# Attention and feed-forward layer on one core: three jobs of exponentials kept in SBUF during the lead-in, with V made afterwards

## The chip, the cores and the metric

The kernel runs on one core of a Trainium2 chip. The metric is the device time of one execution in microseconds (us). Engines are named as in the profile: PE is TensorE (PEld its weight loads), ACT is ScalarE, DVE is VectorE, POOL is GpSimd, SP the engine that issues the DMAs.

## What is computed

A transformer layer in bfloat16, 2048 tokens, model width 1024, 32 heads of 32, hidden width 3584:

```python
x  = A_x                                            # [1, 2048, 1024]
qkv = layernorm(x) @ wqkv                           # no affine part in the norm
p  = softmax(q @ k.T * 32 ** -0.5)                  # per head, all 2048 keys, no mask
h  = x + (p @ v) @ wo
h2 = h + gelu(layernorm(h) @ w1 + b1) @ w2 + b2     # gelu by tanh
```

## The kernel before

**Tasks and a planner.** The Python code adds tasks to a graph (`Graph.add`): each has an engine, the instructions it emits, a planned duration (`occ`), a latency until its result can be used (`lat`), buffers read and written, a priority and a kind. `Graph.schedule` plays the graph through with these durations and so fixes, before the run, the order of instructions on every engine; on the chip each engine works through its list in order and waits on semaphores. PE's next task is chosen by `pick_pe`: score matmuls (`qk`) first, then PV and its sums where enough rounds wait (`PV_FORCE`, `PV_START`), then everything else (`bg`: projections, output projection, feed-forward), by order of creation. Other engines take the ready task with the lowest priority number, then the earliest created. A change of the tiling mode of PE (full, row, col) is planned with `switch`. Planned durations are `MM` for a matmul of 512 columns, `c_dve`, `c_dve_ps`, `c_act` and a few literals.

**Attention.** Heads are taken in 8 blocks `g` of four (32 rows or columns of PE each), queries in 8 blocks `qb` of 256. A job is one (qb, g) and has 8 rounds of 256 keys. A round (`Att.qk`, line 769) makes the scores of four heads in two score units of two PSUM banks each; two ACTIVATEs of 1024 elements (line 779) write their exponentials to one of NR = 9 buffers PT. `Job.pv` (line 805) multiplies V by them into the left half of a bank, DVE adds the two key halves of a PT buffer (a pair sum, PS, line 820, three buffers), and `Job.den` (line 834) sums over the keys with a matmul by ones. `Job.finish` (lines 850 to 865) divides and writes one block of OT. In all there are 64 jobs, 512 rounds and 1024 exponentials.

**Lead-in.** x comes in 16 tiles of 128 tokens; in 8 steps `hc` of two tiles: layer norm on DVE and POOL (lines 583 to 598), transposes on PE (line 604), copy to xnT on ACT (line 611) or DVE (line 613), then Q (for hc < 2) and K of block 0 for these 256 tokens (`proj_half`), V of blocks 0 and 1 (`proj_v`, line 706), and the rounds of jobs (0,0) and (1,0) that have become possible. In this stage the scores use two units (banks 0 to 3); the two jobs hold banks 5 and 6, and the projections share banks 4 and 7. PV follows two rounds behind (`LEAD_LAG`), and these two jobs sum directly from PT, without pair sums. 80 matmuls with no use for the result (line 1007, kind `warm`) are there for moments in which PE has nothing else.

**Afterwards** there are three score units (banks 0 to 5), and jobs and projections share banks 6 and 7 (`slot`). For each g from 1 to 7: Q of query chunk 0, K of all tokens, V of a later block (`rest_of_projections`), then jobs (0,g) and (1,g), and for g in `EXTRA` also (2,g). K and Q go through DVE (line 654). Then follow the rest of Q (`late_q`), and for each query block the output projection `wo`, `ln2`, `ffn1`, `gelu`, `ffn2`, with the jobs three query blocks ahead between them. `wo(u)` needs all eight jobs of query block u, and its first matmul uses g = 7. The last query block is a tail after all attention. Most full-width matmuls are recorded at lines 534 (four column tiles) and 537 (whole), those of the tail at line 540. Line 558 issues nearly all DMAs.

## Time and profile before

| | |
|---|---|
| device time, 3 runs | median 1102.87 us (1101.98 to 1104.28) |
| span of the profiled execution, first to last instruction | 1099.2 us |
| busy: PE, DVE, ACT, POOL | 1056.5, 757.2, 1019.8, 47.8 us |
| exponentials (line 779) | 1024, 953.6 us busy |
| DMA | 174.43 MB, mean 159 GB/s |

The profiled execution is one run of the program. Its own time is its span and what lies around the first and the last instruction; the page gives the span alone, and the median of the runs lies 3.7 us above that. A busy time counts overlapping instructions of an engine once, so that a matmul that waits in the pipeline counts as busy PE; the mean duration of one instruction is its latency, and can be longer than its distance to the next.

### The profile page before, as it was taken

Reading aid. Unit: us, or ns where it says so; the run is one execution under the profiler, and the core shown is the slowest. Engines: PE = TensorE matmul, PEld = TensorE weight load, DVE = VectorE, ACT = ScalarE, POOL = GpSimd, SP = SyncE. Lnnn points to the kernel's source line nnn. Section 1 sums busy time; section 2 is a strip of 40 time slices with the busy share of each in tenths; the row PEclk is TensorE's granted clock in tenths of the full one; section 3 lists DMA queues with packets and bytes.
Section 4 is the critical chain, followed back from the end, with each engine's and each line's share of the span. In section 5 each row is a group of like instructions: output and inputs, shape, how many; then the busy total and the mean of one; then the engine's idle time right before and its main releaser. Section 6 shows DMA issues by size and latency. Waiting matters only on the chain.

```text
span 1099.2 us, 42056 instructions
## 1 busy us (share of the span) xinstructions
PE 1056.5 (96%) x19177; PEld 613.8 (56%) x19226; DVE 757.2 (69%) x1444; ACT 1019.8 (93%) x1124; POOL 47.8 (4%) x110
## 2 busy tenths in 40 slices
PE   8899999998899999999999899999999999999998
PEld 6655555553345744664475456546744664565483
DVE  7746666665676886788588768876886787687501
ACT  3879999999999999999999999999999999999650
POOL 3200000000000001001000100010010000000100
PEclk9999999999899999999999999999999999999999
DMA  6820000048345654854576466448654747797370
GB/s 184 227 103 2 29 2 3 2 159 268 115 122 154 189 151 150 260 162 149 185 228 188 150 203 180 143 150 255 181 178 149 216 142 239 243 266 242 98 262 20
DMA packets 265506, 174.43 MB, mean 159 GB/s; under 512 B 26864, under 2 KB 260336, under 8 KB 264560
## 3 DMA queue, kind: packets, MB, share of 16 engines
q1 hardware_dynamic: 265328, 171.74, 51.2%
q8 instruction: 151, 2.47, 0.9%
q14 instruction: 27, 0.22, 0.1%
HBM read 161.23 MB, written 10.49 MB: 156 GB/s over the span
## 4 chain that ended last, share of the span: by engine, by line
ACT 79%; PE 19%; DVE 1%; issue 0%; DMA 0%; POOL 0%; POOLq 0%; DVEq 0%
ACT PT L779 75%; PE ps L540 6%; ACT uu L965 4%; PE ps L537 4%; PE ps L534 3%; PE ps L769 2%; PE ps L805 1%; PE ps L1007 1%; PE ps L834 1%; DMA a_w1r<-in_A_wo_dram 0%; ACT xnT L611 0%; PE ps L604 0%; DVE PS L820 0%; DVE OD L850 0%; DVE OD L857 0%
## 5 line engine op out<-in xcount | busy, mean ns | idle before, releaser
L779 ACT ACTIVATE PT<-ps 128x1024 bf16<-128x1024 f32 x1024 | 953.6, 1189 | 18.2 <-PE ps L769 18.0
L820 DVE TENSOR_TENSOR PS<-PT 128x1024 bf16<-128x1024 bf16 x434 | 287.5, 686 | 124.5 <-ACT PT L779 63.8
L769 PE MATMUL ps<-QT,KT 32*128 32x256 bf16 x4096 | 204.6, 273 | 13.5 <-ACT PT L779 10.2
L805 PE MATMUL ps<-PT,V 128*32 128x256 bf16 x4096 | 179.9, 273 | 1.5 <-ACT PT L779 1.1
L769 PEld LDWEIGHTS ps<-QT,KT 32*128 32x128 bf16 x4096 | 61.0, 92 | 174.1 <-ACT PT L779 165.3
L834 PE MATMUL ps<-PS,ones 128*32 128x256 bf16 x1736 | 121.7, 274 | 2.0 <-DVE PS L820 2.0
L805 PEld LDWEIGHTS ps<-PT,V 128*32 128x32 bf16 x4096 | 103.8, 97 | 30.0 <-issue 8.7
L537 PE MATMUL ps<-a_w2r,gT 128*128 128x512 bf16 x445 | 109.6, 380 | 4.9 <-issue 2.4
L537 PE MATMUL ps<-hnT,a_w1r 128*128 128x256 bf16 x903 | 111.2, 273 | 1.1 <-DVE rr L860 0.5
L534 PE MATMUL ps<-hnT,a_w1r 128*32 128x256 bf16 x2660 | 96.9, 274 | 2.4 <-DVE gT L943 1.2
L537 PEld LDWEIGHTS ps<-hnT,a_w1r 128*128 128x128 bf16 x903 | 82.7, 98 | 25.1 <-issue 14.8
L943 DVE TENSOR_TENSOR gT<-ps,b1f 128x512 bf16<-128x512 f32 x98 | 67.3, 687 | 27.7 <-PE ps L534 18.4
L534 PE MATMUL ps<-a_w2r,gT 128*32 128x512 bf16 x1140 | 81.6, 381 | 2.5 <-DVE OD L857 2.5
L534 PEld LDWEIGHTS ps<-hnT,a_w1r 128*32 128x32 bf16 x2660 | 66.2, 96 | 18.5 <-issue 14.0
L537 PEld LDWEIGHTS ps<-a_w2r,gT 128*128 128x128 bf16 x471 | 40.4, 98 | 55.3 <-issue 15.7
L989 DVE SCALAR_TENSOR_TENSOR hch<-ps,hch 128x512 bf16<-128x512 f32 x32 | 22.0, 689 | 64.0 <-PE ps L540 47.1
L834 PEld LDWEIGHTS ps<-PS,ones 128*32 128x32 bf16 x1736 | 45.9, 96 | 22.8 <-issue 8.7
L965 ACT ACTIVATE uu<-uu 128x1024 bf16<-128x1024 bf16 x49 | 58.0, 1206 | 0.0
L537 PE MATMUL ps<-xnT,Wall 128*128 128x512 bf16 (+1 forms) x213 | 47.7, 360 | 2.3 <-issue 1.1
L588 POOL CAST mvb<-mv 128x2 bf16<-128x2 f32 (+1 forms) x25 | 6.1, 242 | 990.0 <-DVE mv L585 987.2
L706 DVE CAST V<-ps 128x512 bf16<-128x512 f32 x32 | 22.1, 690 | 30.8 <-PE ps L537 15.8
L537 PE MATMUL ps<-Wall,xnT 128*128 128x256 bf16 x327 | 41.0, 273 | 0.0
(85 smaller groups left out, 1009.8 us busy)
## 6 DMA issues: line engine op xcount, KB each, us to landing
a_w2r<-in_B_w_dram SPq DMA_DIRECT2D x105, 512.0 KB, 5.6
a_w1r<-in_B_w_dram SPq DMA_DIRECT2D x98, 512.0 KB, 4.4
a_w1r<-in_A_wo_dram SPq DMA_DIRECT2D x32, 512.0 KB, 4.0
b_w1r<-in_B_w_dram SPq DMA_DIRECT2D x14, 512.0 KB, 5.8
a_w1r<-in_A_wqkv_dram SPq DMA_DIRECT2D x11, 512.0 KB, 4.3
xrb<-in_A_x_dram SPq DMA_DIRECT2D x16, 256.0 KB, 4.2
Wall<-in_A_wqkv_dram SPq DMA_DIRECT2D x16, 256.0 KB, 4.8
hch<-in_A_x_dram SPq DMA_DIRECT2D x16, 256.0 KB, 4.0
```

Source lines behind the costliest of these rows:

```text
L534: fns.append(lambda p, j=j: p.matmul(psum[32 * j:32 * j + 32, bi(bank), c0:c1], lhsT[:, 32 * j:32 * j + 32], rhs, start=start, stop=stop, ...
L537: t.whole = lambda p: p.matmul(psum[:, bi(bank), c0:c1], lhsT, rhs, start=start, stop=stop, skip_group_check=True)
L540: t = pe(lambda p: p.matmul(psum[:, bi(bank), c0:c1], lhsT, rhs, start=start, stop=stop), occ, reads=reads, writes=[bb(bank)], mode="full" ...
L706: t = dve(lambda v: v.tensor_copy(dst, psum[:, bi(bank), :].rearrange("p (t g c) -> p g t c", t=2, g=2)), c_dve_ps(512), reads=[bb(bank)], ...
L769: return p.matmul(psum[:, 2 * us[h // 2] + h % 2, 256 * i:256 * i + 256], KT[32 * h:32 * h + 32, g, k0:k0 + P], QT[32 * h:32 * h + 32, qs, :],
L779: act(lambda a, u=u, k=k: a.activation(PT[:, s, k, :, :], psum[:, 2 * u:2 * u + 2, :], ACT.Exp, bias=0.0, scale=SCALE), 1024, reads=[B_ps[ ...
L805: fns.append(lambda p, i=i, h=h: p.matmul(psum[32 * h:32 * h + 32, bi(bank), 0:256], V[:, g, 2 * r + i, 32 * h:32 * h + 32], PT[:, s, h // ...
L820: dve(lambda v: v.tensor_tensor(PS[:, n, :, :], pairs[:, :, 0:256], pairs[:, :, 256:512], ALU.add), c_dve(1024, 2), reads=[B_PT[2 * s], B_ ...
L834: fns.append(lambda p, h=h, rhs=rhs, i=i: p.matmul(psum[32 * h:32 * h + 32, bi(bank), 256:512], ones32[:, :], rhs, start=False, stop=last, ...
L943: t = dve(lambda v: v.tensor_tensor(g[:, fc:fc + 2, :], psum[:, bi(bank), :].rearrange("p (f c) -> p f c", f=2), b1f[:, fc:fc + 2].unsquee ...
L965: act(lambda a: a.activation(w, w, ACT.Tanh, bias=0.0, scale=KT2), 1024, reads=[B_uu[i]], writes=[B_uu[i]], prio=-1)
L989: drop(dve(lambda v, hs=hs, bank=bank, half=half: v.scalar_tensor_tensor(hch[:, hs, c], psum[:, bi(bank), :], half, hch[:, hs, c], ALU.mul ...
```

## The change

The lead-in now works on three jobs, (0,0), (1,0) and (2,0), with three score units from the start, and makes only scores and exponentials. V of block 0 is made in four slots of four tiles (`proj_v1`), and PV of these jobs is held back until the last of them is cast (`gate`); their pair sums wait for the last DVE task of the lead-in (`hold`). The exponentials of the 24 rounds stay in SBUF: eight in PT, sixteen in further buffers (`extra_pt`) that lie where K and V of blocks 2 to 5, V of block 1 and weight blocks 5, 3 and 1 go later, and in free space. ACT copies tiles 0 to 3 to xnT and DVE the other twelve; before, ACT copied tiles 0 to 8, 10, 12 and 14. V of block 1 is made in `rest_of_projections(1)`, after `gate`. `EXTRA` becomes [1, 2], so that (2,1) comes early too, as (2,2) did. All lead-in jobs use pair sums for seven of their eight rounds. The order in which two V weight loads stand in SP's list changes, and most of the planner's durations and latencies get other values.

```diff
-    def schedule(self, pick_pe, pool, switch=0.1, dma_rate=280.0, dma_lat=2.1, dma_issue=0.06):
+    def schedule(self, pick_pe, pool, switch=0.104, dma_rate=280.0, dma_lat=2.1, dma_issue=0.06):
...
+    PTs = [PT[:, i] for i in range(NR)]
+    B_PTs = [B_PT[2 * i:2 * i + 2] for i in range(NR)]
...
+    def extra_pt(off):
+        i = len(PTs)
+        h, b = sb(Area(off), "PX%d" % i, [P, 2, 2, 512], BF, 2)
+        PTs.append(h)
+        B_PTs.append(b)
+
+    for g in (2, 3, 4, 5):
+        extra_pt(B_KT[8 * g].lo)
+        extra_pt(B_V[NT * g].lo)
+    for k in (5, 3, 1):
+        extra_pt(B_W[k][0].lo)
+        extra_pt(B_W[k][0].lo + 4096)
+    extra_pt(ph0.cur)
+    extra_pt(B_V[NT].lo)
...
-    MM = 0.2195
+    MM = 0.21333
     def c_dve_ps(n):
-        return (120 + n) / 960.0 + 0.02
+        return (120 + n) / 960.0 - 0.058
     def c_dve(n, x=1):
-        return (62 + n / x) / 960.0 + 0.085
+        return (62 + n / x) / 960.0
     def c_act(n, ap_bias=False):
-        return 0.073 + (0.093 if ap_bias else 0.0) + n / 1200.0
+        return (0.064 if n == 1024 else 0.073) + (0.093 if ap_bias else 0.0) + n / 1200.0
...
-        occ = MM * (c1 - c0) / 512.0 + 0.003
+        occ = MM * (c1 - c0) / 512.0 + 0.0026
...
-            if r == 7 or (self.g == 0 and self.qb < 2):
+            if r == 7:
                 self.sums.append((s, True))
...
-                    reads=[B_PT[2 * s], B_PT[2 * s + 1]], writes=[B_PS[n]], prio=-2)
+                    reads=B_PTs[s], writes=[B_PS[n]], prio=-2, after=hold if self.g == 0 and self.qb < NLJ else ())
...
-    load_w(WV, -5, 0, 256)
     for tt in range(4, 8):
         x_tile(tt, -5)
+    load_w(WV, -5, 0, P)
...
-    LEAD_LAG = 2
-    lead_jobs = [Job(0, 0, 6), Job(1, 0, 5)]
-    att.n_units = 2
+    LEAD_ACT = (0, 1, 2, 3)
+    NLJ = 3
...
-            tr_tile(tt, lead_slot(), "dve" if tt >= 8 and tt % 2 else "act")
+            tr_tile(tt, slot(), "act" if tt in LEAD_ACT else "dve")
...
     for hc in range(8):
         ev = "act" if hc == 0 else "dve"
-        if hc < 2:
-            proj_half(0, hc, lead_slot(), ev)
-        proj_half(1, hc, lead_slot(), ev)
-        first = [t for t in gr.tasks if t.kind == "bg"][-1:] if hc == 0 else ()
+        if hc < NLJ:
+            proj_half(0, hc, slot(), ev)
+        proj_half(1, hc, slot(), ev)
         if hc < 7:
             lead_norm(hc + 1)
-        proj_v(2 * hc, 0, lead_slot(), ev, first)
-        for k, r in {0: [(0, 0)], 1: [(0, 1), (1, 0), (1, 1)]}.get(hc, [(0, hc), (1, hc)]):
-            s = att.qk((k, 0), r)
-            pending.append((lead_jobs[k], r, s))
-            attention_drain(LEAD_LAG)
-    attention_drain()
-    att.n_units = 3
...
+        for k, r in [(k, hc) for k in range(min(hc, NLJ))] + ([(hc, r) for r in range(hc + 1)] if hc < NLJ else []):
+            n = 8 * k + r
+            s = NR + 15 if n == 0 else n - 1 if n < 9 else n
+            lead_rounds.append((k, r, att.qk((k, 0), r, s)))
+    att.rounds = 8
+    hold = [t for t in gr.tasks if t.eng == E.DVE][-1:]
+    for c in range(4):
+        proj_v1(4 * c, 0, 4, slot(), "dve", 0, True)
+    gate = gr.tasks[-1]
+    for k in range(NLJ):
+        job = Job(k, 0, slot(2))
+        for _, r, s in [x for x in lead_rounds if x[0] == k]:
+            job.pv(r, s)
...
+        if g == 1:
+            for c in range(4):
+                proj_v1(4 * c, 1, 4, slot(), "dve", 0, True, [gate])
+        if g in EXTRA:
+            proj(0, g, 1, slot(), "dve")
...
-    EXTRA = [2]
+    EXTRA = [1, 2]
...
-    attention(2, [g for g in range(G) if g not in EXTRA])
+    attention(2, [g for g in range(1, G) if g not in EXTRA])
...
     def ready_rounds(now):
...
+        if gate.done is None or gate.done > now + 1e-9:
+            return 0
```

## The prediction

> **What bounds the kernel now.** I read the page first, then the busy time by stretch, the chain of waits, and the lead-in by form and in order of time.

> ```profile
> span 1099.2 us, 42056 instructions
> ...
> PE 1056.5 (96%) x19177; PEld 613.8 (56%) x19226; DVE 757.2 (69%) x1444; ACT 1019.8 (93%) x1124; POOL 47.8 (4%) x110
> ...
> ACT 79%; PE 19%; DVE 1%; issue 0%; DMA 0%; POOL 0%; POOLq 0%; DVEq 0%
> ```

> ACT carries 79% of the chain that ends last. Where it does not is read from the stretches (all engines, then the exponentials of line 779 alone):

> ```profile
> 0.00:23.00 23.00, 20.13 (x176) 16.11 (x177) 15.39 (x35) 7.97 (x9) 8.60 (x26) 1.00 0.78 206
> 23.00:71.20 48.20, 43.83 (x1059) 30.51 (x1058) 31.21 (x72) 35.88 (x38) 9.07 (x20) 1.00 0.67 194
> 71.20:272.00 200.80, 196.06 (x3598) 109.72 (x3610) 125.08 (x225) 200.79 (x220) 0.00 (x0) 1.00 0.19 59
> 285.00:1031.00 746.00, 722.16 (x13812) 414.15 (x13840) 567.49 (x1079) 743.60 (x809) 26.72 (x56) 1.00 0.61 185
> 1031.00:1099.20 68.20, 64.77 (x434) 40.29 (x439) 11.49 (x23) 19.43 (x37) 3.40 (x8) 1.00 0.37 125
> ...
> 0.00:23.00 23.00, 1.94 (x2) 1.00 0.78 206
> 23.00:71.20 48.20, 29.35 (x30) 1.00 0.67 194
> ```

> The columns are PE, PEld, DVE, ACT, POOL, granted clock, DMA share, GB/s. From 71.2 to 1031 ACT is busy almost throughout. Two stretches are left: the lead-in to 71.2, in which ACT finishes only 32 exponentials (2 + 30), and the 68.2 us tail of feed-forward matmuls, which the change leaves alone. In the middle PE has almost as little room as ACT: 722.2 of 746 us. So ACT sets the pace and PE is close behind. Both matter below.

> The profiled execution has a span of 1099.2 us; the median of the runs is 1102.87, so 3.7 us are added to every span below.

> **The lead-in on ACT.** The chain of waits, and ACT in order of time:

> ```profile
> 71.21 208.25 ACT PT L779 x227
> ...
> 16.40 1.94 ACT L779 ACTIVATE PT<-ps 128x1024 bf16<-128x1024 f32 x2 [0.62 <-PE ps L769]
> 19.97 1.02 ACT L611 ACTIVATE xnT<-ps 128x1024 bf16<-128x1024 bf16 x1 [0.71 <-PE ps L604]
> 24.82 1.02 ACT L779 ACTIVATE PT<-ps 128x1024 bf16<-128x1024 f32 x1 [3.82 <-PE ps L769]
> 40.49 1.94 ACT L779 ACTIVATE PT<-ps 128x1024 bf16<-128x1024 f32 x2 [0.51 <-PE ps L769]
> ```

> Back to back, one exponential takes 208.25/227 = 0.917 us, a round of two 1.834. In the lead-in ACT waits about 0.51 us for the scores before a round (two score units, both occupied), and it also copies transposed tiles: 12 of them, 12.2 us in the row further down.

> After the change ACT keeps tiles 0 to 3 (4 copies, all done by 21 us in the trace of before) and the score units become three, as they are already from 71.2 on, where no such wait is left. The first round can hardly move from 16.4 us, since it hangs on the first two x tiles. The second key chunk came at 24.8; with V's matmuls out of the way I put it at 23, an estimate. From there ACT has 48 − 2 = 46 exponentials and no copy: 46 × 0.917 = 42.2 us, so three jobs are done at 65.2. At 71.2 that makes 48 + 6.0/0.917 = 54.5 exponentials against 32. The 22.5 more are worth 22.5 × 0.917 = **20.6 us**, if ACT is fed without a gap.

> [...] The trace has 0.917, and the sum goes by that.

> **Can DVE feed it?** The lead-in by form, up to 71.2 us:

> ```profile
> L583 DVE BATCH_NORM_STATS2 st<-xrb 128x6 f32<-128x512 bf16 x32 | 21.2, 671 | 4.3 <-DMA xrb<-in_A_x_dram 4.3
> L598 DVE TENSOR_SCALAR xb<-xrb,mvr,rden 128x1024 bf16<-128x1024 bf16 x16 | 8.0, 534 | 0.6 <-POOL rden L594 0.5
> L706 DVE CAST V<-ps 128x512 bf16<-128x512 f32 x8 | 5.5, 690 | 11.1 <-PE ps L534 5.9 <-PE ps L537 5.1
> L585 DVE BATCH_NORM_AGGREGATE mv<-st 128x2 f32<-128x12 f32 x16 | 3.3, 207 | 0.4
> L743 DVE CAST KT<-ps 128x256 bf16<-128x256 f32 x7 | 3.0, 425 | 5.0 <-PE ps L534 4.3 <-PE ps L537 0.5
> L613 DVE COPY xnT<-ps 128x1024 bf16<-128x1024 bf16 x4 | 2.8, 688 | 0.4 <-PE ps L604 0.2
> L611 ACT ACTIVATE xnT<-ps 128x1024 bf16<-128x1024 bf16 x12 | 12.2, 1034 | 10.1 <-PE ps L604 10.1
> ```

> Layer norms: 21.2 + 8.0 + 3.3 = 32.5 us, and about 1 for the small casts. Copies: 12 × 0.688 = 8.3 instead of 4. K and Q casts of block 0: 9 × 0.425 = 3.8. Together 45.6, and 4.3 us of waiting for x, so the last key chunk is ready at 50 us at the earliest. If four V casts and five casts of block 1's Q and K (9 × 0.69 = 6.2) fall in between, at 56. ACT needs that chunk for its last six exponentials, at 65.2 − 5.5 = 59.7. So moving eight copies to DVE costs nothing as long as DVE stays under 59.7; the cover is some 4 us, and each microsecond beyond it is lost on ACT.

> **Handing over to block 1.** From the page, from SP's queue, and PE in the middle of the projections:

> ```profile
> L820 DVE TENSOR_TENSOR PS<-PT 128x1024 bf16<-128x1024 bf16 x434 | 287.5, 686 | 124.5 <-ACT PT L779 63.8
> ...
> 29.76 20.92 SPq L558 DMA_DIRECT2D Wall<-in_A_wqkv_dram  x17
> ...
> 180.48 0.40 PE L769 MATMUL ps<-QT,KT 32*128 32x256 bf16 x8
> 180.81 1.68 PE L537 MATMUL ps<-xnT,Wall 128*128 128x512 bf16 x7
> 182.43 0.40 PE L769 MATMUL ps<-QT,KT 32*128 32x256 bf16 x8
> ```

> Block 1's weights are issued from 29.8 us on, and the lead-in now has no PV and only a little V to hold up PE, so its Q and K can be done before 65. Behind the last V cast wait 24 rounds of PV, and the pair sums wait for the last K cast of the lead-in; what queues behind both is the sums' matmuls on PE and the closings on DVE, and the projections of block 1 that need a bank. The rounds are bound by DVE: 21 pair sums (seven a job) of 0.686 = 14.4 us, and three closings. Meanwhile two jobs hold banks 6 and 7, and the third takes the first that is freed. If V is complete at 57, projections get a bank at about 69 and both at 75. V of block 1 is 32 matmuls' worth of 512 columns; seven such take 1.68 us in the row above, and a following score matmul starts 0.10 us after the last, so about 0.217 each, 6.9 us in all, with half of PE free 13 us: ready at 82. ACT goes on without it for as long as PT has buffers, 9 rounds × 1.834 = 16.5 us, to 81.7. Bounds: 0 (V of block 1 gets in early) and 6 us (it starts only at 75). I take **2 us**, nearer to zero because the two times all but meet.

> SP's queue: V's weights change place with x tiles, and blocks 1, 3 and 5 of the weights wait for their place in SBUF to be read out by PV, at about 75 us; they are for blocks 4 to 7, over 90 us later (a block is two jobs, 29.3 us). I cost both at nothing.

> **PE from the first output projection on.** PE in order of time, then two stretches:

> ```profile
> 277.67 0.61 PE L769 MATMUL ps<-QT,KT 32*128 32x256 bf16 x8 [0.30 <-ACT PT L779]
> 279.50 0.61 PE L769 MATMUL ps<-QT,KT 32*128 32x256 bf16 x8 [1.22 <-ACT PT L779]
> 280.05 2.31 PE L537 MATMUL ps<-a_w1r,OT 128*128 128x512 bf16 x5
> ...
> 275.00:280.00 5.00, 2.67 (x52) 0.86 (x52) 2.81 (x7) 5.00 (x6) 0.00 (x0) 0.76 0.48 144
> 280.00:285.00 5.00, 5.00 (x24) 1.50 (x20) 1.98 (x3) 4.13 (x5) 0.00 (x0) 0.56 0.01 3
> ```

> Here PE ran out of projections and idled until job (0,7) was complete, for only then can the output projection start. Before that point lie 16 jobs; with three early jobs of block row 2 they are 18. Before: 71.2 + 14 × 14.67 = 276.6, first matmul at 280.05. After: 65.2 + 15 × 14.67 = 285.3, so 288.7. PE starts its long part 8.7 us **later**. It then has 16 rounds less beside it. A round takes PE 0.43 (scores with both changes of mode) + 0.22 (PV, as many columns as one matmul of 512 in 0.217) + 0.11 (pair sums, half of that), 0.77 us: 16 × 0.77 = 12.3. At an unchanged pace PE would be only 3.6 us earlier at the end, and ACT's gain needs 17 us more from PE's 746.

> Is that there? Rows of the stretch 285 to 1031:

> ```profile
> L769 PE MATMUL ps<-QT,KT 32*128 32x256 bf16 x3040 | 151.4, 273 | 8.1 <-ACT PT L779 6.2
> L537 PE MATMUL ps<-hnT,a_w1r 128*128 128x256 bf16 x903 | 111.2, 273 | 1.1 <-DVE rr L860 0.5 <-DVE OD L857 0.3
> L537 PE MATMUL ps<-a_w2r,gT 128*128 128x512 bf16 x441 | 108.6, 380 | 4.9 <-issue 2.4 <-DVE gT L967 1.1 <-DVE hch L989 0.7
> L534 PE MATMUL ps<-hnT,a_w1r 128*32 128x256 bf16 x2660 | 96.9, 274 | 2.4 <-DVE gT L943 1.2 <-issue 1.0
> L534 PE MATMUL ps<-a_w2r,gT 128*32 128x512 bf16 x1140 | 81.6, 381 | 2.5 <-DVE OD L857 2.5
> ```

> PE's visible idle is 746 − 722.2 = 23.8 us, 8.1 of it before score matmuls. The order is computed with 0.2195 + 0.003 us for a matmul of 512 columns, and it takes 0.217; these rows hold about 451 + 441 + 332 + 285 = 1509 of them, so the order leaves 1509 × 0.0055 = 8.3 us unused, and the new number (0.2159) fills that. The change of mode is planned at 0.104, close to what the rows show. So 8 to 17 of the 17 us can be found. I take 13, between the two, and lose **4 us**. ACT's shift of durations itself (0.926 planned, 0.917 measured) costs no instruction and I give it nothing.

> Pair sums instead of direct sums for two lead-in jobs save PE 14 × 0.11 = 1.5 us; it lies in the slack above.

> Sum: 1099.2 − 20.6 + 2 + 4 = 1084.6; with 3.7, **1088 us**.

> **The rivals.**
> 1. *ACT alone decides.* PE finds all 17 us and the handover costs nothing: 1078.6 + 3.7 = 1082. For it: 23.8 us of visible idle. Against: these lie scattered, and some wait for DVE. Chance 0.21.
> 2. *PE becomes the bound.* Nothing is found: 1099.2 − 3.6 + 3.7 = 1099. For it: PE already 97% busy there. Against: the 8.1 us in which PE waits for ACT vanish by themselves when ACT is ahead. Chance 0.14.
> 3. *Bank lock-out, slower.* Block 1's Q and K do not get through the two banks before the backlog of PV takes both. ACT then has nothing from 65.2 until a bank frees at 69 and Q and the first K are made (2 × 1.75 us and casts): 75, 10 us. V of block 1 comes after K, at about 95, and PT is full at 91.5: 4 more. PE idling in that time comes back at half clock, as at 280 to 285 (0.56): Q, K and V of block 1, 5 × 1.74 + 6.9 = 15.6 us, take up to twice as long, 10 us of it uncovered. 24 + 4 (PE) − 20.6 = 7 slower: 1110. It decides from 20.6 − 4 = 16.6 us of ACT drought on. Against: weights are there from 30 us. Chance 0.17. [...]

> That lead-in buffers in KT and V delay block 2's projections is part of rival 3's mechanism and not counted again.

> **How the numbers follow.** Forecast (1084 to 1095) 0.45, rivals 0.21, 0.14 and 0.17, and 0.03 that cases cancel to no change. About 2.2 us (0.2%) is what a measurement here can tell from none. Faster 0.45 + 0.21 + 0.14 = 0.80, same 0.03, slower 0.17. The range goes from just under rival 1 (1079) to the line of no change (1102); it leaves out rival 3 and little else.

> **What would show it.** Right: three exponential jobs done at about 65 us, ACT without gaps of 0.5 us before rounds from 24 us on; 4 copies on line 611 and 12 on line 613; first output-projection matmul near 289; last exponential at 1010 to 1018; PE idle between there smaller than 23.8 us. Wrong: ACT idle of over 5 us between 60 and 100, granted clock under 1 in that place, or the last exponential later than 1027.

## The result, and the profile after

The kernel after takes 1095.81 us (median of 5 runs, 1094.16 to 1097.30) against 1102.87 for the kernel before (1101.97 to 1107.64): ratio 0.9936, 95% interval 0.9913 to 0.9959, so it is faster by 7 us, and not by the 15 us of the forecast. The profiled execution took 1094.8 us, 1.8 more than its span. From its page:

```profile
span 1093.0 us, 42528 instructions
...
PE 1052.0 (96%) x19410; PEld 617.4 (56%) x19462; DVE 762.7 (70%) x1467; ACT 1013.7 (93%) x1116; POOL 47.6 (4%) x110
...
ACT 58%; PE 35%; DVE 4%; issue 1%; DMA 1%; POOL 1%; POOLq 0%; DVEq 0%
```

ACT's share of the chain that ends last fell from 79% to 58%, and PE's rose from 19% to 35%: the pace is now set by both. The stretches of after (columns as before), then the exponentials of line 792 alone:

```profile
0.00:23.00 23.00, 19.82 (x192) 15.40 (x196) 18.30 (x44) 9.04 (x11) 10.42 (x30) 1.00 0.78 207
23.00:71.60 48.60, 43.33 (x791) 28.73 (x793) 43.88 (x89) 48.57 (x53) 7.29 (x16) 1.00 0.47 148
71.60:77.00 5.40, 5.01 (x22) 1.89 (x24) 3.63 (x11) 0.00 (x0) 0.00 (x0) 0.68 0.98 223
77.00:272.00 195.00, 190.54 (x3916) 112.59 (x3928) 121.25 (x220) 194.87 (x213) 0.00 (x0) 1.00 0.17 54
285.00:1020.30 735.30, 711.98 (x13922) 412.10 (x13950) 557.87 (x1070) 730.51 (x794) 26.47 (x56) 1.00 0.63 191
1020.30:1093.00 72.70, 69.02 (x450) 42.19 (x453) 11.45 (x23) 19.35 (x36) 3.45 (x8) 1.00 0.39 128
...
0.00:23.00 23.00, 3.22 (x4) 1.00 0.78 207
23.00:71.60 48.60, 48.57 (x53) 1.00 0.47 148
```

From 23 to 71.6 us ACT is busy 48.57 of 48.60 us, with nothing but exponentials. Then it does nothing for 5.4 us, at a PE clock of 0.68, and the tail has become longer: 72.7 us instead of 68.2. ACT and PE at the handover, in order of time:

```profile
21.83 3.77 ACT L792 ACTIVATE PT<-ps 128x1024 bf16<-128x1024 f32 x4 [3.02 <-PE ps L781]
...
63.92 7.65 ACT L792 ACTIVATE PT<-ps 128x1024 bf16<-128x1024 f32 x8
77.03 1.94 ACT L792 ACTIVATE PT<-ps 128x1024 bf16<-128x1024 f32 x2 [5.46 <-PE ps L781]
...
71.99 4.66 PE L549 MATMUL ps<-xnT,Wall 128*128 128x512 bf16 x13 [2.19 <-DVE rr L873]
```

From 21.83 to 63.92 ACT makes the lead-in's other 46 exponentials, 0.915 us each, and the three jobs are done there, at 64. The eight from 63.92 on are block 1's first. By 71.57 ACT has finished 56 exponentials, by 71.2 in the kernel before 32. What is then missing is the next scores: K of block 1 (line 549, xnT and Wall) waits for a PSUM bank until a lead-in job is closed (line 873).

**The account.** I add up, between successive instructions of ACT, the distance from start to start beyond 0.918 us, wherever it is over 0.06 us, and call it ACT's loss. The time is then the end of the last exponential plus the tail behind it.

| us | before | after | difference |
|---|---|---|---|
| lead-in: 24 exponentials more, less 0.4 us of time | | | −21.6 |
| ACT's loss 69 to 110 (the handover) | 0.2 | 6.2 | +6.0 |
| ACT's loss 110 to 300 | 3.0 | 3.9 | +0.9 |
| ACT's loss from 300 to the last exponential | 5.8 | 9.0 | +3.2 |
| left over (pace of an exponential) | | | +0.7 |
| last exponential ends | 1031.1 | 1020.3 | −10.8 |
| tail | 68.1 | 72.7 | +4.6 |
| span | 1099.2 | 1093.0 | −6.2 |

The first row counts 56 exponentials by 71.57 us against 32 by 71.2. The tail is longer because feed-forward work is left over when the attention is done. PE's groups in the tail, first of before, then of after:

```profile
L537 PE MATMUL ps<-a_w2r,gT 128*128 128x512 bf16 x4 | 1.0, 379 | 0.0
```
```profile
L549 PE MATMUL ps<-a_w2r,gT 128*128 128x512 bf16 x25 | 6.0, 379 | 0.1
```

These matmuls of the second feed-forward product are those that were meant to lie beside the last jobs; 21 more of them at 0.217 us are 4.6 us, the whole difference.

### The profile page after: what moved, and what is told of

The parts are those of the page before. It is cut to its first block, busy times and chain, and to the rows that moved or that the text cites. A ratio compares the mean times of both kernels' runs of the same rounds, so it can differ in the third digit from the quotient of the medians.

```text
span 1093.0 us, 42528 instructions
## 1 busy us (share of the span) xinstructions
PE 1052.0 (96%) x19410; PEld 617.4 (56%) x19462; DVE 762.7 (70%) x1467; ACT 1013.7 (93%) x1116; POOL 47.6 (4%) x110
## 4 chain that ended last, share of the span: by engine, by line
ACT 58%; PE 35%; DVE 4%; issue 1%; DMA 1%; POOL 1%; POOLq 0%; DVEq 0%
ACT PT L792 53%; PE ps L549 11%; PE ps L546 8%; PE ps L552 6%; PE ps L781 5%; PE ps L818 3%; ACT PX L792 3%; ACT uu L978 2%; PE ps L847 2%; DVE PS L833 1%; DMA q_scratch<-lq 1%; DVE st L595 1%; DVE gT L956 1%; DVE lq L703 0%; POOL denb L604 0%
## 5 line engine op out<-in xcount | busy, mean ns | idle before, releaser
L792 ACT ACTIVATE PT<-ps 128x1024 bf16<-128x1024 f32 x992 | 921.4, 1090 | 15.0 <-PE ps L781 14.5
L818 PE MATMUL ps<-PT,V 128*32 128x256 bf16 x3968 | 174.3, 273 | 1.7 <-ACT PT L792 0.9
L546 PE MATMUL ps<-hnT,a_w1r 128*32 128x256 bf16 x2904 | 103.7, 274 | 5.2 <-DVE gT L956 1.7
L549 PE MATMUL ps<-hnT,a_w1r 128*128 128x256 bf16 x842 | 103.2, 273 | 0.7 <-DVE OD L870 0.2
L549 PE MATMUL ps<-a_w2r,gT 128*128 128x512 bf16 x396 | 97.0, 380 | 6.0 <-issue 2.0
L546 PE MATMUL ps<-a_w2r,gT 128*32 128x512 bf16 x1340 | 97.8, 381 | 0.5 <-DVE hch L1002 0.5
L549 PEld LDWEIGHTS ps<-hnT,a_w1r 128*128 128x128 bf16 x842 | 77.2, 98 | 22.5 <-issue 12.9
L546 PEld LDWEIGHTS ps<-hnT,a_w1r 128*32 128x32 bf16 x2904 | 71.8, 96 | 24.2 <-issue 16.9
L956 DVE TENSOR_TENSOR gT<-ps,b1f 128x512 bf16<-128x512 f32 x98 | 67.3, 687 | 20.4 <-PE ps L546 13.2
L549 PE MATMUL ps<-xnT,Wall 128*128 128x512 bf16 (+1 forms) x256 | 55.2, 352 | 4.4 <-DVE rr L873 2.8
L549 PE MATMUL ps<-Wall,xnT 128*128 128x128 bf16 (+1 forms) x443 | 43.9, 247 | 0.0
L546 PEld LDWEIGHTS ps<-a_w2r,gT 128*32 128x32 bf16 x1340 | 29.4, 96 | 23.7 <-issue 15.2
```

The costliest lines, as they stand in the source:

```text
L546: fns.append(lambda p, j=j: p.matmul(psum[32 * j:32 * j + 32, bi(bank), c0:c1], lhsT[:, 32 * j:32 * j + 32], rhs, start=start, stop=stop, ...
L549: t.whole = lambda p: p.matmul(psum[:, bi(bank), c0:c1], lhsT, rhs, start=start, stop=stop, skip_group_check=True)
L792: act(lambda a, u=u, k=k: a.activation(PTs[s][:, k, :, :], psum[:, 2 * u:2 * u + 2, :], ACT.Exp, bias=0.0, scale=SCALE), 1024, reads=[B_ps ...
L818: fns.append(lambda p, i=i, h=h: p.matmul(psum[32 * h:32 * h + 32, bi(bank), 0:256], V[:, g, 2 * r + i, 32 * h:32 * h + 32], PTs[s][:, h / ...
L956: t = dve(lambda v: v.tensor_tensor(g[:, fc:fc + 2, :], psum[:, bi(bank), :].rearrange("p (f c) -> p f c", f=2), b1f[:, fc:fc + 2].unsquee ...
```

## The experiments

"Loss 20–110" and "loss 300–980" are ACT's losses as above; span, last exponential and tail are those of the profiled execution. Each ratio is to the kernel before on the same chip.

| run | median us | ratio (95%) | loss 20–110 | loss 300–980 | last exp. | tail |
|---|---|---|---|---|---|---|
| before | 1102.87 | | 11.9 | 5.5 | 1031.1 | 68.1 |
| after | 1095.81 | 0.9936 (0.9913–0.9959) | 6.5 | 8.7 | 1020.3 | 72.7 |
| e1 durations alone | 1107.38 | 1.0048 (1.0032–1.0064) | 10.2 | 13.0 | 1038.2 | 69.7 |
| e2 one early job less | 1101.44 | 0.9997 (0.9982–1.0012) | 14.3 | 13.2 | 1032.3 | 66.5 |
| e3 one bank | 1095.10 | 0.9937 (0.9918–0.9957) | 3.9 | 9.1 | 1018.0 | 73.1 |
| e4 less ffn2 | 1096.42 | 0.9951 (0.9932–0.9970) | 6.5 | 14.0 | 1027.5 | 69.0 |
| e5 old PE numbers | 1105.14 | 1.0041 (1.0026–1.0057) | 7.4 | 9.0 | 1021.0 | 81.0 |
| e6 old PE and DVE numbers | 1117.01 | 1.0132 (1.0115–1.0150) | 11.1 | 8.4 | 1022.1 | 93.2 |
| e7 ffn1 whole | 1097.24 | 0.9959 (0.9946–0.9973) | 6.1 | 4.5 | 1016.0 | 80.1 |
| e8 direct sums | 1096.58 | 0.9956 (0.9943–0.9970) | 7.1 | 9.2 | 1020.7 | 73.0 |
| e9 two lead-in jobs | 1104.07 | 1.0021 (1.0005–1.0037) | 13.2 | 14.4 | 1034.0 | 67.9 |
| e10 one bank, quarter whole | 1089.28 | 0.9880 (0.9859–0.9901) | 4.3 | 5.1 | 1015.3 | 72.2 |
| e11 after again | 1096.81 | 0.9956 (0.9943–0.9970) | 6.3 | 10.0 | 1022.9 | 72.8 |
| e12 quarter whole alone | 1095.18 | 0.9942 (0.9924–0.9960) | 6.7 | 9.5 | 1021.5 | 72.2 |
| e13 after, shifted 128 | 1096.95 | 0.9958 (0.9945–0.9971) | 6.0 | 10.8 | 1021.9 | 72.8 |
| e14 after, shifted 64 | 1096.64 | 0.9956 (0.9942–0.9970) | 6.7 | 9.9 | 1021.9 | 72.8 |
| e15 e10, shifted 128 | 1094.30 | 0.9929 (0.9915–0.9943) | 5.2 | 9.2 | 1020.8 | 72.1 |
| e16 e10, shifted 64 | 1089.09 | 0.9891 (0.9875–0.9907) | 5.4 | 5.3 | 1015.3 | 72.1 |

**What the lead-in's parts are worth: e9 and e2.** e9 is after with two lead-in jobs:

```diff
-    NLJ = 3
+    NLJ = 2
...
-    attention(2, [g for g in range(1, G) if g not in EXTRA])
+    attention(2, [g for g in range(G) if g not in EXTRA])
```

> The kernel after with two lead-in jobs instead of three; job (2,0) goes back to the later place of row 2. Theory (the lead-in's gain of 21.6 us is work found for ACT while it waits for keys, and the third job is most of it): the third job is 16 exponentials x 0.917 = 14.7 us, of which block 1 can take back only what it starts earlier; ACT loses 10 to 14 us more before 110 us, the last exponential ends at about 1030, the tail shrinks from 72.7 to about 68 because PE's background work gets that time, span about 1098, ratio to before 0.996 to 1.000. Rival (two jobs with three score units and no V or PV in the lead-in are enough, the third only brings the 6 us gap at the handover): ACT loses less than 5 us more before 110 us, gap at the handover under 2 us, span 1090 to 1093.

It loses the whole gain, but not all of it in the lead-in. ACT's group of e9 from 20 to 72 us, and one of its waits in order of time:

```profile
L792 ACT ACTIVATE PT<-ps 128x1024 bf16<-128x1024 f32 x28 | 26.7, 1026 | 14.4 <-PE ps L781 14.3
...
60.16 3.77 ACT L792 ACTIVATE PT<-ps 128x1024 bf16<-128x1024 f32 x4 [4.51 <-PE ps L781]
```

Of the 14.4 us, 3.0 lie before 21.8, as in after. With two jobs ACT then waits 5.8 us for the last four key chunks, and, with both jobs done at 55.7, 5.5 us for block 1's scores: the third job fills these 11.3 us and brings the gap at the handover. At 300 us ACT has finished 279 exponentials in before, 287 in e9 and 295 in after, so that half of the lead is there with two jobs; the rival, by which the third job brings only the gap, is wrong. What e9 had won it loses behind 300 us, where ACT's loss is 14.4 us instead of 5.5 in before (8.7 in after); 5.5 of them lie at four pauses of the kind told of further down. So the span (1101.9, expected 1098) does not say what the third job alone is worth.

e2 takes away job (2,1), the new early job:

```diff
-    EXTRA = [1, 2]
+    EXTRA = [2]
```

> The changed kernel with EXTRA = [2], so job (2,1) is not early; (2,0) and (2,2) still are. Theory A (the end is the start of the first output projection plus a PE-bound phase): that start, now at 296 us, comes about 14.7 us earlier, less an ACT gap of some 8 us near 98 us because block 2 is not ready; the PE phase has 8 rounds more, 8 x 0.77 = 6.2 us. Net about 0: 1095 to 1097, with the first output projection near 289. Theory B (ACT gaps add up directly): the 8 us gap is lost, 1103.

ACT then has a second gap, 7.91 us before 106.9. By then it has made 80 exponentials, three lead-in jobs and two of block 1, so block 2's scores are what it waits for: the early job covers block 2's projections. At 300 us ACT is at 287 exponentials, as in e9, and from there on it loses 4.5 us more than after, 2.0 of them because it has four pauses and after two. In time nothing is left of the gain, and the expectation of about no change against after (theory A) missed; theory B, by which the gap counts in full, came nearer.

**What holds up the handover: e3 and e8.** e3 lets the lead-in jobs use bank 6 alone, so that bank 7 stays free for block 1's projections; e8 lets them sum straight from the exponentials, so that DVE has no backlog of pair sums.

```diff
-        job = Job(k, 0, slot(2))
+        job = Job(k, 0, Slot(gr.buf(), 2, (6,)))
```

> The changed kernel, but the three lead-in jobs may only take bank 6, so bank 7 stays with the projections while the PV backlog runs. If the 5.5 us gap of ACT at 71.6 us comes from both banks being held by jobs (block 1's third key chunk has no bank), the gap shrinks to 2 us or less or moves behind 80 us, granted clock stays at 1.00 there, the first output projection comes 3 to 5 us earlier and the time falls by as much: 1091 to 1093. If the gap comes from DVE (pair sums) or from late weights, it stays at about 5 us and the time stays at 1096.

```diff
-            if r == 7:
+            if r == 7 or (self.g == 0 and self.qb < NLJ):
```

> The changed kernel with the lead-in jobs summing directly from PT, as before the change: 21 pair sums of 0.62 us apart go from DVE, 21 x 0.11 = 2.3 us are added on PE. Theory G (the gap at 71.6 us is a DVE-bound backlog that holds both banks): the backlog ends 6 us or more earlier, the gap at 72 us goes, as it did with one bank (to 3 us in two or three pieces), and the time falls by 2 to 4 us, 1092 to 1094. Theory H (what is won at the handover is given back later, as with one bank): the gap goes and the time stays at 1095 to 1096.

ACT of e3 at the handover:

```profile
82.81 1.94 ACT L792 ACTIVATE PT<-ps 128x1024 bf16<-128x1024 f32 x2 [1.99 <-PE ps L818]
85.66 23.34 ACT L792 ACTIVATE PT<-ps 128x1024 bf16<-128x1024 f32 x25 [0.91 <-PE ps L781]
```

With one bank there is no gap at 72 us. Two smaller ones of 2.9 us together come later: the first waits for PV (line 818), the second is a pause of PE of the kind told of further down. The loss from 69 to 110 is 3.6 us instead of 6.2. With direct sums that loss is 6.6 us, no smaller, but it is another one. ACT of e8, then PE of e8:

```profile
64.45 16.69 ACT L792 ACTIVATE PT<-ps 128x1024 bf16<-128x1024 f32 x18
85.87 1.94 ACT L792 ACTIVATE PT<-ps 128x1024 bf16<-128x1024 f32 x2 [4.73 <-PE ps L818]
```
```profile
85.14 0.46 PE L546 MATMUL ps<-Wall,xnT 128*32 128x128 bf16 x20 [2.37 <-issue]
```

The gap at 72 us is gone here too, as theory G had it: ACT works on to 81.1. Then all nine PT buffers are full (18 exponentials, as in e3), and it waits until V of block 1 lets PV read one of them; PE's making of V (Wall and xnT) is itself held up by a pause of 2.37 us. That the time stays is as theory H had it. So two things together make the gap of after: lead-in jobs hold both banks, and they hold them because their closing comes behind pair sums on DVE. DVE of after:

```profile
62.56 6.67 DVE L833 TENSOR_TENSOR PS<-PX 128x1024 bf16<-128x1024 bf16 x11
69.15 1.89 DVE L833 TENSOR_TENSOR PS<-PT 128x1024 bf16<-128x1024 bf16 x3
70.95 0.44 DVE L863 STREAM_TRANSPOSE OD<-ps 128x256 f32<-128x256 f32 x1
```

To free one bank (e3) or to take the pair sums away (e8) removes it, and the next wait, for V of block 1 at full PT buffers, then shows. It is 1.99 us in e3; of the 4.73 us in e8 the pause is 2.37. That the last exponential ends 2.3 us earlier in e3 cannot be told from after in the device time.

**Are the planned durations a cost or a gain: e1, e5, e6.** e1 is the kernel before with the new durations and nothing else; e5 is after with the old numbers for PE, e6 with those for PE and DVE.

```diff
-    MM = 0.2195
+    MM = 0.21333
...
-            pe(fns, 0.224, reads=[B_KT[8 * g + r], B_QT[qs]], writes=banks, kind="qk", mode="row")
+            pe(fns, 0.222, reads=[B_KT[8 * g + r], B_QT[qs]], writes=banks, kind="qk", mode="row")
```

> The kernel before, with only the planner's durations, latencies and mode-switch cost of the change; lead-in, jobs and bank use stay as they were. Theory A (PE is the second bound, and what the new durations give is a denser order of PE after the first output projection): the span falls by part of PE's idle time, 3 to 8 us, so about 1095 to 1100. Theory B (ACT alone bounds, durations change nothing that ACT waits for): within 2 us of 1102.9. Theory C (the new durations are tighter than the chip, so instructions come later than planned and ACT starves): slower, above 1105.

> The changed kernel with the planner's PE numbers of before (matmul 0.2195 + 0.003, mode switch 0.1, PE latency 0.16, and those of score, PV, sum, transpose and warm-up matmuls); ACT's and DVE's stay new. Theory D (the new PE numbers cost time on the chip, as they did alone, by 5 us): 1088 to 1092, with the ACT time lost between 300 and 980 us going from 8.7 towards 5.5 us. Theory A (the new numbers fill PE's idle time and help): slower than the changed kernel by 5 to 10 us, 1100 to 1105.

> As e5, and DVE's numbers of before too; only those of ACT stay new. Theory D, where it is the whole set that costs 5 us: 1088 to 1091 like e5 or better. Theory E (only DVE's numbers matter in the lead-in, where they shape the handover): ACT's gap near 72 us changes place and size, up to 8 us, and the time is 1096 to 1100.

The same numbers go with opposite results. In after the old ones for PE leave the last exponential where it is (1021.0) and make the tail 81.0 us: the order leaves PE's work behind. PE's group in e5's tail, to be read against the 25 above:

```profile
L549 PE MATMUL ps<-a_w2r,gT 128*128 128x512 bf16 x62 | 14.0, 379 | 0.0
```

e5 came out as its theory A had it. e6, with DVE's old numbers too, has the last exponential at 1022.1 and a tail of 93.2 us; both of its theories missed.

In before the new numbers cost 5 us, as in theory C. PE is ahead there, and runs out of work before the attention ends. Two stretches of e1, then one of before:

```profile
1020.00:1030.00 10.00, 6.37 (x104) 2.52 (x104) 4.41 (x10) 10.00 (x12) 0.00 (x0) 0.61 0.19 55
1030.00:1040.00 10.00, 7.59 (x93) 2.17 (x90) 2.77 (x4) 7.82 (x9) 0.00 (x0) 0.67 0.19 55
```
```profile
1020.00:1030.00 10.00, 9.84 (x204) 5.22 (x201) 6.14 (x13) 10.00 (x11) 0.00 (x0) 1.00 0.19 62
```

PE's clock is 0.61 and 0.67 where it was 1.00. But ACT is busy 10.00 of 10.00 us in the first of these stretches, and its loss from 980 us to the last exponential is 0.9 us (0.3 in before): the lack of work at the end hardly costs time. The time is lost earlier, 13.0 us instead of 5.5 from 300 to 980. At the four pauses of the kind told of below ACT loses 5.7 us, at the one of before 1.2, so that 4.5 of the 7.5 us more are theirs. Whether the durations cost anything apart from the pauses, e1 does not tell.

**Is PE now the bound: e4 and e7.** e4 leaves 96 matmuls of the second feed-forward product out (query blocks 0 to 5); e7 makes the first one whole instead of in four column tiles.

```diff
-            for fc in range(FC):
+            for fc in range(FC if u > 5 else FC - 4):
```

> The changed kernel, leaving out 4 of the 28 hidden blocks in the second feed-forward matmul of query blocks 0 to 5 (96 matmuls of 512 columns, 96 x 0.217 = 20.8 us of PE, nothing of ACT, and the loads stay). Theory A (PE is the bound after the first output projection): the time falls until ACT binds, by 6 to 10 us, and the stretch from the last exponential to the end goes from 72.7 back to about 68 us: 1086 to 1090. Theory B (ACT is the bound): at most 2 us, 1094 to 1096.

```diff
-                       [R.B_w1[s]] + B_hnT, not tail, (256 * f, 256 * f + 256))
+                       [R.B_w1[s]] + B_hnT, False, (256 * f, 256 * f + 256))
```

> The changed kernel with the first feed-forward matmul always as one instruction of 128 columns instead of four of 32. All pauses of PE of 0.8 us and more that wait for nothing in the profile (1.43 and 1.64 us here, 1.0 to 1.6 in the others) lie in stretches of four-fold matmuls of 256 columns, which take eight instructions in 0.11 us. Theory F (PE's instructions are not there in time in such stretches): no such pause is left in 300 to 980 us, ACT loses 3.8 us less there; against that more mode switches, some 0.2 us in each round with PV and feed-forward, which only costs where PE has no room: 1090 to 1097. Other theory (the pauses come from DMA traffic or are chance): pauses of the same number and length stay.

e4 removes 96 × 0.217 = 20.8 us of PE's work, and the time does not fall. The tail goes down to 69.0, but ACT loses 5.3 us more between 300 and 980: its four pauses cost ACT 5.9 us (after's two 3.6), and PE also waits for DVE, 1.19 us at 593.89. PE runs dry at the end as in e1 (its clock is 0.54 from 1010 to 1020). So "PE is the bound" is wrong as it stood: with less work PE did not keep ACT fed any better.

e7 was to test the pauses of PE that wait for nothing visible. In after there are two of 0.8 us or more from 300 us on. PE at the first, PE at the second, and ACT behind the first:

```profile
463.46 0.29 PE L847 MATMUL ps<-PS,ones 128*32 128x256 bf16 x2 [1.43 <-issue]
...
799.08 0.40 PE L546 MATMUL ps<-hnT,a_w1r 128*32 128x256 bf16 x7 [1.64 <-issue]
...
464.89 5.65 ACT L792 ACTIVATE PT<-ps 128x1024 bf16<-128x1024 f32 x6 [1.49 <-PE ps L781]
```

ACT loses 1.7 and 1.9 us at them. A matmul in four column tiles is four instructions, and four weight loads, for the same work: from 300 us on after has 842 of the first feed-forward product whole and 2904 in tiles, and 842 + 2904/4 are e7's 1568. Whole, there is no such pause and ACT loses 4.5 us instead of 8.7. The group of e7 from 295 to 1015 us:

```profile
L552 PE MATMUL ps<-hnT,a_w1r 128*128 128x256 bf16 x1568 | 201.5, 274 | 3.3 <-DVE gT L956 2.7
```

But the tail grows to 80.1: what ACT won, PE lost. A change between whole, row-tiled and column-tiled work costs PE time: in after, from 300 to 980 us, the next matmul starts 0.205 us after one of 256 columns instead of 0.109. Between 300 and 980 us e7 has 795 such changes and after 694, so an estimate of 101 × 0.096 = 9.7 us.

**A quarter whole: e10, e11, e12.** e12 makes every fourth block whole, and e10 does this and has the one bank of e3; e11 is after once more.

```diff
-                       [R.B_w1[s]] + B_hnT, not tail, (256 * f, 256 * f + 256))
+                       [R.B_w1[s]] + B_hnT, not tail and blk % 4 > 0, (256 * f, 256 * f + 256))
```

> The kernel after with two edits: lead-in jobs keep to bank 6 (as in the run with one bank, gap at the handover 3.6 us), and every fourth block of the first feed-forward matmul is whole instead of in four column tiles, so that no stretch of four-fold 256-column matmuls is longer than three blocks. Theory (PE's pauses come when a long stretch of four-fold matmuls uses up the instructions that have been fetched): pauses of 0.8 us and more go or get shorter, ACT loses 5 to 7 us instead of 8.7 between 300 and 980, the whole blocks cost few changes of mode, span 1086 to 1090. Rival (pauses do not hang on the length of the stretch, or each microsecond won on ACT comes back as a longer tail): span 1091 to 1094, as with one bank alone.

> The kernel after unchanged, beside the two others on the same chip, to see how far its span, its gap at the handover and its two pauses of PE repeat. If the order fixes them: last exponential 1019 to 1022, tail 72 to 74, handover gap 5 to 6 us, pauses at about 463 and 799 us. If pauses are chance: same times at the handover, but pauses at other places, and up to 2 us of difference in the last exponential.

> The kernel after with the second edit of the run before alone: every fourth block of the first feed-forward matmul whole, lead-in jobs as in after. Theory (the stop of PE costs time on both engines, so taking it away is a net gain, and the bank at the handover is a separate, smaller item): no pause of 0.8 us and more between 300 and 980 us, ACT loses 4.5 to 6.5 us there, handover gap as in after (6 us of loss between 69 and 110), last exponential about 1017, tail 72 to 73, span about 1089.5, 3 to 6 us under after. Rival (the gain of the run before needed both edits, since either one alone only turns ACT's gain into a longer tail): span 1092 to 1095, tail 75 or more.

e10 beats both kernels: 1089.28 us, no pause between 300 and 980, and the tail not longer. e12 gives nothing, and its expectation missed: two pauses remain, at 406 and 863, neither of them where after had one. e11 has after's pauses again, at 465.1 and 800.1 (1.80 and 1.15 us): in one and the same kernel their places repeat. So the length of column-tiled stretches is not what decides.

**The border of the instruction transfers: e13 to e16.** The trace of after shows one queue of the kind "instruction" with 152 transfers of 16384 bytes, and 39,000 instructions of PE: one transfer for every 257, or 64 bytes for each. That these transfers bring PE's instructions is an estimate from the two counts. Of the 47 pauses of 0.8 us or more that wait for nothing visible, in all runs together, 45 end 2.2 to 2.7 us after the start of such a transfer, and these transfers came late: in all 45, PE began 307 to 501 instructions between the end of the transfer before and the end of this one, where the median in after is 247. Lateness alone is not enough, for in all runs together 683 transfers came 307 or more instructions later. In after, transfers start at 447.91 and 461.26, with 471 instructions, and PE goes on at 463.46. The four runs shift the border. They cut 64 or 32 of the warm matmuls in the first 12 us in two, which is the same work and the same order, with 128 or 64 PE instructions more ahead of it.

```diff
-        pe(lambda p: p.matmul(psum[:, 6, 0:256], ident[:, :], b2t[:, 0:256], ...
+        pe([lambda p, c=c: p.matmul(psum[:, 6, c:c + 128], ident[:, :], b2t[:, c:c + 128], ...) for c in (0, 128)]
+           if k < 64 else lambda p: p.matmul(psum[:, 6, 0:256], ident[:, :], b2t[:, 0:256], ...
```

> The kernel after, in which 64 of the 80 warm matmuls in the first 12 us are cut into two halves of 128 columns: the same work and the same planned order, and 128 more PE instructions (64 matmuls, 64 weight loads) ahead of all the rest. The traces show PE's instructions coming in transfers of 16384 bytes, 256 instructions each if one is 64 bytes (152 transfers for some 39,000), and every pause with no visible cause of 0.8 us or more starts 1 to 3 us after such a transfer that came late (369 to 490 PE instructions after the one before it). Theory (a pause depends on where the border of a transfer falls in the order): pauses near 463 and 799 us go or change, others appear elsewhere; the last exponential moves by 1 to 4 us from 1020.3 to 1022.9, span 1089 to 1097. Rival (pauses hang on the kind of work at that place, not on the border): pauses at 463 to 466 and 799 to 801 us as before, 1.1 to 1.8 us each, span 1093 to 1096.

> As the run with 128 more instructions, but with 32 warm matmuls cut in two, 64 more PE instructions ahead of the rest. Theory: another set of pauses than with 0 and with 128 more; sum of ACT's losses from 300 to 980 us between 4 and 13 us, and the last exponential moves with it. Rival: the same two pauses, losses 8 to 10 us.

> The fastest kernel so far (lead-in jobs in one bank, every fourth block of the first feed-forward matmul whole, 1089.3 us, no pause between 300 and 980 us) with 128 more PE instructions ahead of the rest, by cutting 64 warm matmuls in two. Theory (its lead over the kernel with the whole blocks alone is mostly a lucky position of the transfers' borders): one to three pauses appear, ACT loses 7 to 11 us instead of 5.1 between 300 and 980, span 1089 to 1093. Rival (the two edits together keep PE from running out of instructions): no pause there, span 1086 to 1089.

> As the run before with 64 more PE instructions instead of 128. Theory: again another set of pauses, span anywhere from 1087 to 1093. Rival: no pause between 300 and 980 us, span 1086 to 1089.

Some of the pauses move. After has them at 463 and 799, shifted by 128 at 465 and 559, by 64 at 862 and 975: with 128 one stays and one goes, with 64 both go. In e10's order there is none from 300 us on; shifted by 128 there is a long one at 830 (with one of 0.79 at 862), by 64 one at 857. Earlier on all three of them have one at 85 us (1.35, 1.97 and 1.90 us), wherever the border lies. PE of e15, then of e16:

```profile
827.90 0.38 PE L818 MATMUL ps<-PT,V 128*32 128x256 bf16 x6
830.04 0.29 PE L818 MATMUL ps<-PT,V 128*32 128x256 bf16 x2 [1.76 <-issue]
```
```profile
857.13 0.40 PE L847 MATMUL ps<-PT,ones 128*32 128x256 bf16 x7 [0.92 <-issue]
```

The pause of e15 splits one PV in the middle, its eight matmuls being six and two, so that it does not begin with a new piece of work. But the places are not arbitrary: of the 18 profiles eight have a pause between 447 and 465 us and eight one between 854 and 863. For these 16 the DMA share in the 3 us ahead of the late transfer was over 1.0. After at its two pauses, the 3 us ahead of the late transfer (the last two columns are DMA share and GB/s):

```profile
458.26:461.26 3.00, 3.00 (x104) 2.13 (x96) 3.00 (x5) 3.00 (x4) 0.00 (x0) 1.00 1.07 366
793.65:796.65 3.00, 3.00 (x108) 2.20 (x99) 3.00 (x7) 3.00 (x4) 0.00 (x0) 1.00 0.66 197
```

In all traces the DMA share in the 3 us ahead was 0.95 or more for 37 of the 45 transfers that ended a pause, for 87 of the 129 that came 400 or more instructions later (counted in the same way), and for 271 of the 1906 that came under 300 later. So full DMA engines go with late transfers, mostly; that they cause them is not shown, for no run changed the DMA traffic.

What the border is worth: the same work in the same order takes 1094.30 us with one border and 1089.09 with another (the intervals of their ratios do not meet), and ACT's loss from 300 to 980, 9.2 against 5.3, accounts for 3.9 of the 5.2 us. In after's order the three borders differ by 1.1 us at most, which the intervals cannot tell apart. So e10's lead over after (1096.81 in e11), 2.5 to 7.7 us with the border, is in part the position of the border; how much the bank and the whole blocks give apart from it, these runs do not settle.

## Why the prediction was half right

**Right: the lead-in on ACT.** Forecast 20.6 us, measured 21.6. The three jobs were done at 64 (forecast 65.2), and ACT started its unbroken stretch at 21.8 (estimate 23). The copies went as said, 4 and 12, and DVE had the room:

```profile
L625 DVE COPY xnT<-ps 128x1024 bf16<-128x1024 bf16 x12 | 8.1, 681 | 1.4 <-PE ps L616 1.3
L623 ACT ACTIVATE xnT<-ps 128x1024 bf16<-128x1024 bf16 x4 | 4.1, 1027 | 7.4 <-PE ps L616 7.4
```

The 46 exponentials from 21.83 to 63.92 took 0.915 us each, close to the 0.917 that the sum went by.

**Mis-sized: the handover, 2 us against 6.** The step that failed is "block 1's Q and K can be done before 65". I looked for the wait at V of block 1; it came at K's third chunk, because the lead-in jobs take banks 6 and 7 before block 1's projections are through: only two of its four chunks were cast by 71.6. That is rival 3's mechanism at a fourth of its price: it has the two parts that the rival named, ACT without work (5.46 us) and PE at a lower clock (0.68 from 71.6 to 77). e3 and e8 show what made it: banks held by jobs whose closing comes behind the pair sums on DVE, for either edit removes the gap. How long the jobs hold them I had nearly right: a bank for the projections at about 69, and it was 72.0. The wait that I had priced at 2 us, V of block 1 at full PT buffers at 81.7, exists as well. It shows where the first gap is gone, from 80.8 on in e3 at 1.99 us; in after the first gap comes before it and hides it. The sign that I had set for "wrong", ACT idle for over 5 us between 60 and 100 at a clock under 1, was there. Of the signs for "right" those of the lead-in came; the first output projection (296.25 us, set near 289) and the last exponential (1020.3, set for 1010 to 1018) came late.

**Mis-sized: PE from the first output projection on, 4 us against 8 to 9.** From that point on it has three parts. First, the starting point: I had 288.7, and it was 296.25.

```profile
295.92 0.40 PE L781 MATMUL ps<-QT,KT 32*128 32x256 bf16 x8 [1.44 <-ACT PT L792]
296.25 1.68 PE L549 MATMUL ps<-a_w1r,OT 128*128 128x512 bf16 x7
...
260.00:280.00 20.00, 16.67 (x281) 6.67 (x277) 10.15 (x21) 18.40 (x21) 0.00 (x0) 0.83 0.70 262
```

The handover (5.5) and ACT's loss of 2.0 us between 270 and 278, where PE itself starves at a clock of 0.57 (0.83 in the row above), explain most of it, less the 1.2 us by which the three jobs ended earlier. Secondly, what PE finds: its long part, from that matmul to the end of the span, took 819.15 us before and 796.75 after, 22.4 less; 12.3 of that are the 16 rounds that are gone, by my estimate of 0.77 us each, so it found 10 of the 17 us, inside my 8 to 17 and below the 13 that I took. That PE's new numbers are where it comes from fits e5: without them the time is 8 to 9 us higher (1105.14 against 1095.81 and 1096.81). Thirdly, what no row of mine held: pauses that go with late instruction transfers, 3.1 us of PE in after, which cost ACT 3.6 us. The kernel before has one in that part of its trace, 1.01 us at 855, and I had added it to "idle that lies scattered". So, as far as these two profiles go, 2 of the 3 us that PE found too little are the pauses.

Seen from PE the whole is a short sum: the long part starts 16.2 us later and is 22.4 us shorter, which is the −6.2 us of the span. My terms were 8.7 and 2 later and 12.3 and 13 shorter, −14.6. Of the 8.4 us between the two, 5.5 are the late start and 2.9 what PE did not find.

By ACT's account the sum with the measured terms is −21.6 + 6.0 + 0.9 + 3.2 + 0.7 + 4.6 = −6.2, against −20.6 + 2 + 4 = −14.6: 1 us better in the first term, 9.4 worse in the others.

**What I gave nothing.** That the durations could do harm by themselves I had not considered; in the kernel before they went with 5 us, most of which lie at pauses (e1). That the pair sums in the lead-in cost no time came out (e8), though there the wait only changes its place. "PE becomes the bound" (rival 2) and "ACT alone" (rival 1) were set as alternatives. Neither holds: less work for PE did not shorten the time (e4), and a smaller loss of ACT came back as a longer tail (e7).

## What to carry to other kernels

Where two engines are both busy 93% of the time or more, a gain on one is worth only what the other can follow, as in e4 and e7: count the time as the end of the last instruction of the first engine plus the tail that the second still has, and look at both before and after. An order computed from planned durations is not always better for truer durations: PE's new numbers went with 8 to 9 us less in one kernel here, and the whole new set with 5 us more in another. When an edit leaves a sum of waits as it was, look at where each wait now stands: the one that was asked about may be gone, and the next have taken its place. And a difference of a few microseconds between two orders of a kernel with 40,000 instructions may be nothing but the place where an instruction transfer falls (e15 has 64 PE instructions more ahead than e16, otherwise the same work in the same order, and takes 1094.30 against 1089.09 us); shift it by a few dozen harmless instructions and measure again, before it is put down to the change.
